# Interleaving the 128 rows of each streamed weight block's DRAM copy by sixteen

## The chip, the cores and the metric

The kernel runs on one core of one Trainium2 chip. The metric is device time in microseconds (us) of one execution. The kernel before was timed three times; the median is 1813.09 us.

## What is computed

Two blocks share the input `x` (2048 rows of 1024, bf16), after one layer norm, and their results are added to it:

```python
xn = _layernorm(x, axis=-1)
return x + _A_ref(xn, A_mem0, A_Wq, A_Wk, A_Wv, A_Wo, A_seg_len) + _B_ref(xn, ...)
```

Block A cuts the 2048 rows into 64 segments of 32. In front of each segment stand 8 rows of memory. The 40 rows go through attention with 32 heads of 128 (projections `Wq`, `Wk`, `Wv` of 1024 x 4096 each, then `Wo` of 4096 x 1024). The first 8 rows of the result are the memory of the next segment, so the 64 segments are a chain. Block B picks the two rows of `xn` with the largest product with `w_r`, runs them through a gated feed-forward layer (1024 to 3584 and back), and adds the result to these two rows.

## The kernel before

**The weights as granules.** The four matrices of block A are cut into 64 granules of 128 partitions x 2048 bf16 values (512 KB). Granules 0 to 47 hold 128 rows of half of `Wq`, `Wk` or `Wv`; granules 48 to 63 hold two heads of `Wo`. Every segment needs all 64 in a fixed order. 44 of them stay in SBUF (`resident`), three more are kept in PSUM and other corners (`KEPT_HERE`), and 17 are fetched again in each segment: the list `streamed` on line 80. One of these, granule 58 (`PART`), has 320 of its columns at home, so 432 KB of it travel.

**The copies.** In the original matrices a row of a granule is a piece of a longer row, or two pieces. So during segment 0 the program copies each streamed granule once, DRAM to DRAM, to a tile of its own, `wsc[g]` (line 123), whose 128 rows of 4,096 bytes lie one behind the other. `copy_block` (lines 442 to 444) issues these copies from GpSimd (POOL): six granules inside phase 1 of segment 0 (line 840), six after phase 1 and the last five after phase 2 (line 616).

**The stream.** `fetch` (lines 399 to 413) takes the next granule off the list `flow`, takes one of five slots (`wstream`, `N_SLOT = 5`) and issues one DMA from SyncE (SP) into it: in segment 0 from the original matrix, afterwards from `wsc[g]` (lines 407 and 412). `after` (line 622) calls `fetch` when TensorE (PE) has been given the last matmul that reads a streamed granule. The DMA waits until that granule's slot has been read, and for an earlier DMA of the same semaphore.

**One segment.** Lines 814 to 831 project the 32 rows that depend on the chain: six phases of eight granules, four matmuls of 128 x 512 each (line 821). Transposes, scores, softmax and attention are hooked in between. Lines 882 to 903 multiply with `Wo` (line 876). Besides the stream, GpSimd issues a few small transfers in each segment: the segment's rows of `x` (`XN`, line 354), queries, keys and values of the memory rows that were worked out ahead (`QKL`, line 637; `VL`, line 642), partial results (`ol_d`, line 664) and the output (line 909).

**Transfers of the form that the change brings in.** Three loads already read DRAM with 16 as the outer count and 8 rows inside, into 128 partitions: `left_rows` (line 223, tile `XLR`, at the start) and `load_left_x` (line 652, tile `XLS`, in the last segment), both 16 x 8 rows of 2,048 bytes of `x`, and `load_vl` (line 642, with two more from SP on line 588), 16 x 8 pieces of `vl_d`. In all three the sixteen groups stand 64 KB apart in DRAM, and the eight rows of a group follow each other.

Of the kernel before, what the change touches and what calls it, by code (L numbers as in the profile page):

```python
# [8 lines left out]
BF16 = mybir.dt.bfloat16  # L9
# [13 lines left out]
PART, AT_HOME = 58, 320  # L23
# [8 lines left out]
def kernel(  # L32
# [16 lines left out]
    nc = tc.nc  # L49
    P = 128  # L50
    Bsz, S, D = A_x.shape
# [28 lines left out]
    streamed = [1, 4, 11, 15, 21, 23, 29, 34, 37, 41, 45, 47, 50, 54, 56, 58, 63]  # L80
# [4 lines left out]
    def granule_dram(g):  # L85
        if g < 48:
            p, kc = divmod(g, KC)
            mat, half = PHASES[p]
            return Wqkv[mat][kc * P:(kc + 1) * P, 2048 * half:2048 * (half + 1)]
        w = g - 48  # L90
        return Wo2[2 * w * P:(2 * w + 2) * P, :].rearrange("(hh e) d -> e hh d", hh=2)
# [11 lines left out]
    def granule_out(t, g):  # L103
        return t[:, :] if g < 48 else t.rearrange("p (hh d) -> p hh d", hh=2)
# [3 lines left out]
    dram = ctx.enter_context(tc.tile_pool(name="dram", bufs=1, space=DRAM))  # L108
# [11 lines left out]
    vl_d = [dram.tile([16, 16, XL, 2, P], BF16, name=f"vl_d{t}") for t in range(4)]  # L120
    ol_d = [dram.tile([P, 16, XL * H], BF16, name=f"ol_d{t}") for t in range(4)]

    wsc = {g: dram.tile([P, 2048 - AT_HOME if g == PART else 2048], BF16, name=f"wsc{g}") for g in streamed}
    r_d = dram.tile([1, S], BF16, name="r_d")

    res_tiles = {}
# [4 lines left out]
    def room(g, name):  # L131
        if g not in place:
            return home(g, [P, 2048], BF16, name)[:, :]
        tag, i = place[g]
        return areas[tag][:, i, :]
# [14 lines left out]
    def travelling(g):  # L150
        if g != PART:
            return [(slice(0, 2048), granule_dram(g))]
        w = granule_dram(g)
        return [(slice(0, D - AT_HOME), w[:, 0, AT_HOME:D]), (slice(D - AT_HOME, 2048 - AT_HOME), w[:, 1, :])]
# [44 lines left out]
    for s in range(4):  # L199
        nc.vector.tensor_copy(out=SELM[:, s, 0:XM, :],  # L200
                              in_=IDENT[:, 32 * s:32 * s + XM].unsqueeze(2).to_broadcast([P, XM, 4]))
# [197 lines left out]
    def fetch():  # L399
        if not flow:  # L400
            return
        s, g = flow.pop(0)
        t = wstream.tile([P, 2048], BF16, tag="g", name="g")
        if g == PART and s < NSEG - 1:
            n = 2048 - AT_HOME
            for c, w in travelling(g) if s == 0 else [(slice(0, n), wsc[g][:, :])]:
                nc.sync.dma_start(out=t[:, c], in_=w)
            t = (OP, t)
        elif s == 0 or g == PART:
            nc.sync.dma_start(out=granule_out(t, g), in_=granule_dram(g))  # L410
        else:
            nc.sync.dma_start(out=t[:, :], in_=wsc[g][:, :])
        queued.append((g, t))

    def part(t, jq):
# [25 lines left out]

    def copy_block(g):
        for c, w in travelling(g):
            nc.gpsimd.dma_start(out=wsc[g][:, c] if g == PART else granule_out(wsc[g], g), in_=w)

    to_copy = list(streamed)
    flow += [(s, g) for s in range(NSEG) for g in (streamed if s else first_streamed) if s or g != GUEST]
# [44 lines left out]
    for g in range(KC):  # L492
        if g in first_streamed:
            assert flow.pop(0) == (0, g)
            t = wstream.tile([P, 2048], BF16, tag="g", name="g")
            queued.append((g, t))
        else:
            t = res_tiles[g] = room(g, f"wres{g}")
# [10 lines left out]
    for g in range(KC, 32):  # L509
        if g == GUEST:  # L510
            t = res_tiles[g] = room(v_homes[8], "guest")
            nc.sync.dma_start(out=t, in_=granule_dram(g))
        elif g in first_streamed:
            if len(queued) < N_SLOT:
                fetch()
        else:
            load_resident(g)
        if g >= 8 and g < 15:
            load_x(g - 7)
# [70 lines left out]
    def left_done(p):  # L590
        for g in range(8 * p, 8 * (p + 1)):
            if g in first_streamed and g != GUEST:
                fetch()
        if p == 0:
            sd_rows(MV[:, 1:NT, :], VE[:, 1:NT])
            spread(1, NT)
            router_tiles()
        elif p == 1:
            res_tiles.pop(GUEST)
            load_resident(v_homes[8])  # L600
            area("big0", [P, 8, 2048], "W8A")
            for g in AREAS["big0"]:
                load_resident(g)
        elif p == 2:
            router_top()
            route_rows()
        elif p == 3:
            route_turns(*routed[0])
            load_resident(hx)
            home_first()  # L610
        elif p == 4:
            area("big1", [P, 8, 2048], "W8B")
        elif p == 5:
            load_resident(hm)
        if p in (1, 2):
            copy_blocks(6)

    def copy_blocks(n):
        for _ in range(min(n, len(to_copy))):
            copy_block(to_copy.pop(0))  # L620

    def after(s, g):

        if g in streamed:
            fetch()
        if s == NSEG - 1:
            if g in resident and g < 48 and g not in place and g not in resident[:3]:
                free_homes.append(g)
            if g in (54, 55):
                for t in (2 * g - 108, 2 * g - 107):  # L630
                    load_left_x(t)
            if g >= 57:
                fetch_moe(1)
# [61 lines left out]
    for s in range(NSEG):  # L695
# [118 lines left out]
        for p, (mat, half) in enumerate(PHASES):  # L814
            PSm = psA.tile([P, 512], F32, tag="acc", name="PSm")
            behind = []
            for kc in range(KC):
                g = 8 * p + kc
# [249 lines left out]
```

## Time and profile before

| What | Value |
|---|---|
| three runs, median (lowest, highest) | 1813.09 us (1803.46, 1813.56) |
| the profiled execution, its own time | 1819.23 us |
| span of its instructions | 1817.6 us |
| granted TensorE clock, mean | 0.985 |
| bytes moved by DMA, mean rate | 673.33 MB, 370 GB/s |
| segments 1 to 63 in the trace | about 219 us to 1728 us |

The page's time strip divides the span into 40 equal slices: the first five are the loads and segment 0, the last two the work behind the last segment (block B's matrices and the rows computed ahead), and all between is the chain of segments. "DMA share" in a table of windows is the mean busy share of the core's 16 DMA engines. [...] "To landing" is the time from the issue of a DMA to its completion.

### The profile page before, as it was taken

The page shows a single profiled execution, that of the slowest core. Times are in us where ns is not written, and L with a number is a line of the kernel's source. Part 1 is how long each engine was busy: PE and PEld are TensorE (multiplying, and loading weights), DVE is VectorE, ACT ScalarE, POOL GpSimd, SP SyncE. Part 2 cuts the span into 40 slices and gives each one's busy share as a digit, 9 for nine tenths or more (in the row PEclk, how much of TensorE's full clock was granted, in tenths as well). Part 3 has the DMA queues.
Part 4 walks back from the last instruction along what each step waited for, and adds up shares of the span by engine and source line. Part 5 has one row for each costly group of instructions (what it writes and reads, how often), then busy time and mean ns, then how long its engine had stood idle before and what let it go on. Part 6 is the DMA issues. An engine that isn't in the chain of part 4 may idle for free. (4 is left out here: it accounts for less than half of the span.)

```text
span 1817.6 us, 70275 instructions
## 1 busy us (share of the span) xinstructions
PE 1564.2 (86%) x30261; PEld 840.5 (46%) x30273; DVE 887.0 (49%) x2843; ACT 779.6 (43%) x2027; POOL 330.6 (18%) x610
## 2 busy tenths in 40 slices
PE   8999888888888888888888888888888888888887
PEld 5444344444444444444444444444444444444454
DVE  6822255444555554545555554455555555555531
ACT  3343144444444444444444444444444444444410
POOL 1121311111111111111111111111111111111220
PEclk9999899999999999999999999999999999999999
DMA  9785999999999999999999999999999999999998
GB/s 357 281 291 174 304 366 381 357 384 378 382 387 389 390 397 368 389 388 389 396 387 383 393 381 366 382 396 393 395 394 395 372 388 393 396 394 393 397 379 294
DMA packets 215961, 673.33 MB, mean 370 GB/s; under 512 B 42801, under 2 KB 46433, under 8 KB 215649
## 3 DMA queue, kind: packets, MB, share of 16 engines
q1 hardware_dynamic: 189232, 616.61, 88.9%
q0 software_dynamic: 25392, 50.39, 8.2%
q8 instruction: 236, 3.87, 0.9%
q10 hardware_dynamic: 1024, 1.84, 0.3%
q14 instruction: 77, 0.62, 0.1%
HBM read 647.74 MB, written 29.81 MB: 373 GB/s over the span
## 5 line engine op out<-in xcount | busy, mean ns | idle before, releaser
L821 PE MATMUL PSm<-wres,ST 128*32 128x512 bf16 x6400 | 501.6, 383 | 0.0
L821 PEld LDWEIGHTS <-ST 128*32 128x32 bf16 x12288 | 314.9, 96 | 345.0 <-issue 105.1
L821 PE MATMUL PSm<-g,ST 128*32 128x512 bf16 x3080 | 306.9, 385 | 40.8 <-DMA g<-wsc 36.6
L435 ACT COPY BK<-KEPT 128x512 bf16<-128x512 bf16 x315 | 189.3, 601 | 179.7 <-PE WO L876 68.0
L876 PEld LDWEIGHTS <-OT 128*32 128x32 bf16 x8255 | 218.1, 98 | 85.3 <-issue 67.7
L830 ACT CAST XB<-PSm 128x512 bf16<-128x512 f32 x256 | 150.3, 587 | 116.0 <-PE PSm L821 114.1
L716 DVE COPY KT<-BT 128x512 bf16<-128x512 bf16 x126 | 51.0, 405 | 283.9 <-PE BT L706 283.8
L876 PE MATMUL WO<-W8B,OT 128*32 128x256 bf16 x4096 | 188.2, 279 | 0.0
L821 PE MATMUL PSm<-W8A,ST 128*32 128x512 bf16 x2048 | 182.3, 381 | 0.0
L637 POOL DMA_DIRECT2D QKL<-ql_d x63 | 46.8, 743 | 740.4 <-ACT OTL L789 724.4
L876 PE MATMUL WO<-g,OT 128*32 128x256 bf16 (+1 forms) x2497 | 130.8, 278 | 52.6 <-DMA g<-wsc 44.6
L909 POOL DMA_DIRECT2D out_dram<-XN x256 | 130.4, 517 | 181.2 <-DVE XN L905 168.4
L849 ACT CAST VM<-PSm 128x512 bf16<-128x512 f32 x128 | 79.6, 622 | 99.5 <-PE PSm L821 99.4
L435 DVE COPY BK<-KEPT 128x512 bf16<-128x512 bf16 x189 | 80.2, 424 | 72.6 <-ACT BK L435 36.8
L706 PEld LDWEIGHTS <-XB 128*128 128x128 bf16 x1024 | 57.8, 97 | 105.8 <-ACT XB L830 99.3
L706 PE MATMUL BT<-IDENT,XB 128*128 128x128 bf16 x1024 | 101.6, 222 | 2.5
L733 DVE TENSOR_TENSOR BS<-BS,CT 128x96 f32<-128x96 f32 (+1 forms) x256 | 59.6, 233 | 84.5 <-PE BS L726 80.0
L711 ACT COPY QT<-BT 128x512 bf16<-128x512 bf16 x128 | 75.0, 586 | 58.0 <-PE BT L706 55.6
L821 PE MATMUL PSm<-BK,ST 128*32 128x512 bf16 x567 | 77.0, 391 | 22.1 <-DVE ST L393 22.1
L534 PE MATMUL PSG<-XLT,wres 128*128 128x512 bf16 x336 | 93.1, 379 | 0.8 <-ACT GA L536 0.7
L751 DVE TENSOR_REDUCE DN<-BS 128x8 f32<-128x320 f32 x128 | 62.8, 491 | 60.0 <-ACT BS L743 60.0
L905 DVE CAST XN<-WO 128x256 bf16<-128x256 f32 x64 | 27.2, 424 | 132.8 <-PE WO L876 132.8
(195 smaller groups left out, 2339.1 us busy)
## 6 DMA issues: line engine op xcount, KB each, us to landing
g<-wsc SPq DMA_DIRECT2D x1008, 512.0 KB, 6.3
g<-wsc SPq DMA_DIRECT2D x62, 432.0 KB, 5.7
ql_d<-GA POOLq DMA_DIRECT2D x16, 512.0 KB, 6.7
QKL<-ql_d POOLq DMA_DIRECT2D x63, 128.0 KB, 6.3
MW<-in_B_w_gate_dram SPq DMA_DIRECT2D x16, 448.0 KB, 13.8
wres<-in_A_Wk_dram SPq DMA_DIRECT2D x12, 512.0 KB, 10.2
MW<-in_B_w_down_dram SPq DMA_DIRECT2D x12, 512.0 KB, 9.1
MW<-in_B_w_up_dram SPq DMA_DIRECT2D x12, 448.0 KB, 9.0
```

The lines of the kernel that those rows point to most:

```text
L435: copy(out=back[g][c], in_=KEPT_COLS[g][c])
L534: nc.tensor.matmul(PSG[:, :], lhsT=part(Gs[kc], h // 4)[:, P * (h % 4):P * (h % 4 + 1)], rhs=XLT[:, :, kc, :], start=(kc == 0), stop=(kc = ...
L706: nc.tensor.transpose(out=PTq[:, il, :, :].rearrange("p j r -> p (j r)"), in_=XB[:, il * P:(il + 1) * P], identity=IDENT[:, :])
L711: nc.scalar.copy(out=QT[half][:, :, :], in_=pv)
L716: (nc.vector.tensor_copy if s else nc.scalar.copy)(out=KT[half][:, :, 0:32], in_=pv)
L733: nc.vector.tensor_tensor(out=S4, in0=S4, in1=m, op=ALU.add)
L751: nc.vector.tensor_reduce(out=DN[:, :], in_=S8, axis=AX.X, op=ALU.add)
L821: nc.tensor.matmul(PSm[32 * jq:32 * jq + 32, :], lhsT=ST[:, kc, :], rhs=part(Gv, jq), start=(kc == 0), stop=(kc == KC - 1), tile_position= ...
L830: nc.scalar.copy(out=XB[:, :], in_=PSm[:, :])
L849: nc.scalar.copy(out=VM[half][:, :], in_=PSm[:, :])
L876: nc.tensor.matmul(PS[32 * g:32 * g + 32, c0:c1], lhsT=lhs(h), rhs=rhs, start=False, stop=(last and hs == 1), tile_position=(0, 32 * g), s ...
L909: nc.gpsimd.dma_start(out=out2[s * SEG:s * SEG + XM, 256 * g:256 * (g + 1)], in_=OB[32 * g:32 * g + XM, :])
```

## The change

Row numbers inside each copy change. The tile of a copy has now the shape 8 x 16 x columns, and all its users see it through a view with 16 in front: partition 8e + i of the granule (e from 0 to 15, i from 0 to 7) is row 16i + e of the copy. Before, partition p was row p. So what stood in eight rows that follow each other stands in eight rows that are 16 rows (64 KB) apart, and the sixteen rows 16i to 16i + 15 belong to sixteen blocks of eight partitions.

```diff
-    wsc = {g: dram.tile([P, 2048 - AT_HOME if g == PART else 2048], BF16, name=f"wsc{g}") for g in streamed}
+    wsc = {g: dram.tile([P // 16, 16, 2048 - AT_HOME if g == PART else 2048], BF16,
+                        name=f"wsc{g}").rearrange("i e c -> e i c") for g in streamed}
...
-            for c, w in travelling(g) if s == 0 else [(slice(0, n), wsc[g][:, :])]:
+            for c, w in travelling(g) if s == 0 else [(slice(0, n), wsc[g])]:
...
-            nc.sync.dma_start(out=t[:, :], in_=wsc[g][:, :])
+            nc.sync.dma_start(out=t[:, :], in_=wsc[g])
...
     def copy_block(g):
         for c, w in travelling(g):
-            nc.gpsimd.dma_start(out=wsc[g][:, c] if g == PART else granule_out(wsc[g], g), in_=w)
+            if g < 48 or g == PART:
+                nc.gpsimd.dma_start(out=wsc[g][:, :, c], in_=w)
+            else:
+                for hh in range(2):
+                    nc.gpsimd.dma_start(out=wsc[g][:, :, D * hh:D * (hh + 1)], in_=w[:, hh, :])
```

No engine's order changes, and all of SP's DMAs stand where they stood. The copies of granules 50, 54, 56 and 63 are two DMAs each where they were one. On GpSimd, in segment 0 behind phase 2, the rows before are these (the last number is the shape of what is written; `wsc_117` to `wsc_121` are the copies of granules 50, 54, 56, 58 and 63):

```order
L316 DMA RT_1345<-in_A_x_dram 1x16x64
L444 DMA wsc_117<-in_A_Wo_dram 256x1x1024
L444 DMA wsc_118<-in_A_Wo_dram 256x1x1024
L444 DMA wsc_119<-in_A_Wo_dram 256x1x1024
L444 DMA wsc_120<-in_A_Wo_dram 128x704
L444 DMA wsc_120<-in_A_Wo_dram 128x1024
L444 DMA wsc_121<-in_A_Wo_dram 256x1x1024
L567 COPY CT<-VG 128x4
```

In the changed program the same place reads:

```order
L317 DMA RT_1345<-in_A_x_dram 1x16x64
L449 DMA wsc_117<-in_A_Wo_dram 16x8x1024 x2
L449 DMA wsc_118<-in_A_Wo_dram 16x8x1024 x2
L449 DMA wsc_119<-in_A_Wo_dram 16x8x1024 x2
L446 DMA wsc_120<-in_A_Wo_dram 16x8x704
L446 DMA wsc_120<-in_A_Wo_dram 16x8x1024
L449 DMA wsc_121<-in_A_Wo_dram 16x8x1024 x2
L572 COPY CT<-VG 128x4
```

Nothing moved past anything else; four DMAs are added in front of the copy to `CT`.

## The prediction

> **What bounds the kernel now.** I read the page first: busy times, the strip by slices and the DMA queues.
>
> ```profile
> PE 1564.2 (86%) x30261; PEld 840.5 (46%) x30273; DVE 887.0 (49%) x2843; ACT 779.6 (43%) x2027; POOL 330.6 (18%) x610
> DMA  9785999999999999999999999999999999999998
> q1 hardware_dynamic: 189232, 616.61, 88.9%
> g<-wsc SPq DMA_DIRECT2D x1008, 512.0 KB, 6.3
> g<-wsc SPq DMA_DIRECT2D x62, 432.0 KB, 5.7
> ```
>
> Two rows run close to full. PE is busy for 86% of the span. The DMA strip shows 9 in every slice of the chain of segments, and SP's queue alone (q1) fills 88.9% of the sixteen engines' time. Of its 616.61 MB, 1008 x 0.524 + 62 x 0.442 = 556 MB are the reads that the change rearranges. To see which of the two ends the segments, I took the table of windows for the whole stretch of reads from the copies, and the waits inside it.
>
> ```profile
> 219.00:1728.00 1509.00, 1285.72 (x28178) 690.34 (x28175) 772.27 (x2569) 702.72 (x1881) 280.01 (x507) 0.99 1.01 386
> PE WO L876 <- DMA g<-wsc: 44.1, 111, 1.6
> PE PSm L821 <- DMA g<-wsc: 36.6, 91, 1.5
> L642 POOL DMA_DIRECT2D VL<-vl_d x63: 532/554/566, 232.4 to 1713.9; - x63
> ```
>
> The last three numbers of the window row are the clock, the DMA share and GB/s: a share of 1.01, so the engines are never out of work for long, at 386 GB/s. PE waits for granules 202 times, 80.7 us in total. The load of VL comes once a segment, so a segment takes (1713.9 - 232.4) / 62 = 23.90 us. It moves 16 x 512 + 432 KB of stream and 128 + 64 + 48 + 64 + 4 x 12 KB of other things, 9.19 MB; at 386 GB/s that is 23.8 us. So bytes over rate gives the segment: **the DMA engines set the pace**, and what the change is worth is what it does to the 386 GB/s. One per cent of the rate is 15 us.
>
> **How much rate there is to win.** I compared stretches of the same trace.
>
> ```profile
> 114.00:120.00 6.00, 5.87 (x53) 2.28 (x52) 0.00 (x0) 3.92 (x6) 0.50 (x1) 1.00 1.03 415
> 1000.00:1006.00 6.00, 5.30 (x112) 2.49 (x108) 1.75 (x6) 2.97 (x6) 1.65 (x3) 1.00 1.03 410
> 1007.00:1011.00 4.00, 3.44 (x88) 1.43 (x80) 3.10 (x11) 1.61 (x4) 0.00 (x0) 1.00 1.02 375
> 1760.00:1783.00 23.00, 22.84 (x154) 14.62 (x156) 1.28 (x2) 1.10 (x4) 0.56 (x1) 1.00 1.03 407
> ```
>
> The first row loads `Wv` from rows 8 KB apart, the fourth block B's matrices from rows 7 KB apart. Neither lies as the copies do, and they run at 415 and 407 GB/s. The second row is the stream from the copies with little beside it: 410 GB/s. The third, in the same segment, is the stream while GpSimd's loads of XN and VL land: 375. So the old layout already reads as fast as any other wherever it is undisturbed. Against the best stretch it lacks 5 of 415, 1.2%, which is 18 us over 1509 us; that is the most that a smoother order could take from quiet stretches. The rest of the way from 386 to 410 is lost beside other transfers, whose layout stays.
>
> **The change part by part.**
>
> *The reads, 1070 of them.* Same bytes, same rows of 4,096 (3,456) bytes, same slots, same waits. What changes is which rows are near each other in time. "The engines read rows that lie together" needs engines that stand at the same row at the same moment. A read lands 6.3 us after its issue, and one is issued every 23.90 / 17 = 1.41 us, so 4.5 are under way at once, and nothing in the program holds the sixteen engines together within them. An engine that is a few rows ahead reads another 64 KB, or another granule. No view shows engine positions, so this is an argument, not a reading. Price, bounded from both sides: -18 us (all of the quiet stretches' lack) to +0 from locality alone. I take 0, since the three layouts above differ by no more than their neighbours do.
>
> [...]
>
> *The issue on SP.* A read whose DRAM side is 16 x 8 needs longer on SP. The trace has the form on lines 588, 223 and 652:
>
> ```profile
> L412 SPq DMA_DIRECT2D g<-wsc x1008: 319/320/1404, 218.9 to 1728.3; - x168
> L588 SPq DMA_DIRECT2D VL<-vl_d x2: 533/538/542, 165.4 to 196.4; - x2
> L223 SPq DMA_DIRECT2D XLR<-in_A_x_dram x2: 573/637/701, 0.9 to 1.7; - x2
> L652 SPq DMA_DIRECT2D XLS<-in_A_x_dram x4: 599/662/870, 1728.7 to 1731.0; - x4
> ```
>
> I take the quiet 538 ns: 0.218 us more for each, 17 x 0.218 = 3.7 us of SP's time in a segment. SP then issues for 17 x 0.538 = 9.1 of 23.9 us, so it does not become a bound. Behind a late read stand only later reads of the stream, and for them waits PE. The cover is the queue: 4.5 reads under way are 6.3 us of work, and a read that enters 0.2 us later finds the engines busy (share 1.01). Cost 0. Without the cover, a slot's cycle of 5 x 1.41 = 7.05 us would grow by 0.218, 3.1%, or 47 us: the upper bound.
>
> *The copies on POOL.* Four DMAs more.
>
> ```profile
> L444 POOL DMA_DIRECT2D wsc<-in_A_Wo_dram x6: 692/940/1147, 129.2 to 131.9; - x6
> L444 POOL DMA_DIRECT2D wsc<-in_A_Wv_dram x5: 517/518/527, 92.5 to 97.7; - x5
> 129.23 3.85 POOL L444 DMA_DIRECT2D wsc<-in_A_Wo_dram  x6
> 158.02 0.19 POOL L567 COPY CT<-VG 128x4 bf16<-128x4 bf16 x1 [24.94 <-DVE PT L749]
> ```
>
> Six issues take 3.85 us; ten of half the pieces take between 10 x 0.518 = 5.2 us and 3.85 + 4 x 1.147 = 8.4 us. POOL's next work stood still for 24.94 us until 158, so 1.4 to 4.6 us disappear there. Cost 0; if the cover were gone, 4.6 us. The copies write the same bytes, and their first reader starts at 219 us, more than 80 us later.
>
> *The work behind the last segment* (40 us) is untouched.
>
> **The sum.** The profiled execution took 1819.23 us, 1.6 us of it outside its span of 1817.6, and stands 0.3% above the median of 1813.09. Terms: reads 0 (-18 to 0), issue 0 (0 to +47), copies 0 (0 to +4.6). So 1819 against its own time, and **1813 us** against the median.
>
> **Rivals.**
>
> *A: the form itself is slow (much slower).* The three transfers of the form 16 x 8 into 128 partitions are also the slow places of the trace:
>
> ```profile
> 4.00:7.00 3.00, 3.00 (x53) 3.00 (x51) 2.32 (x6) 0.00 (x0) 2.04 (x4) 1.00 1.05 253
> 12.00:15.00 3.00, 2.09 (x10) 1.01 (x9) 2.62 (x9) 0.21 (x1) 0.00 (x0) 0.50 1.07 391
> 1737.00:1743.00 6.00, 5.27 (x38) 3.34 (x30) 3.00 (x8) 0.00 (x0) 3.68 (x8) 0.88 1.05 282
> ```
>
> While XLR lands, full engines move 253 GB/s, and right afterwards 391; while XLS lands, 282. If the form does that, for instance because engine e then writes eight partitions in a row and two engines press on the same part of SBUF, every segment pays: 9.19 MB at 282 GB/s are 32.6 us, 8.7 us more, x 63 = +548 us, 2361 us. It decides as soon as the stream falls below PE's own 1285.72 / 63 = 20.4 us a segment, that is 450 GB/s, so at once. Against it: in these transfers the sixteen groups stand 64 KB apart, and after the change neighbouring groups stand 4 KB apart, so distance explains the slow places as well as form; and the slowdown reaches transfers of other forms that run beside them. I keep it at 0.10.
>
> [...]
>
> *B: faster.* The sixteen blocks of a granule now differ in their place inside 64 KB, whatever the engines' positions, the opposite of XLS. If crowding of engines on equal places is part of what slows the disturbed stretches, these get shorter. A third of the way from 386 to 410 GB/s gives 1509 x (1 - 386/394) = 31 us, 1782 us. PE's 80.7 us of waits for granules leave room for that. Against it: the disturbers keep their layout. 0.17.
>
> *C: slower by a little.* The issue time is not covered in the stretches where the queue runs low, or an engine pays for rows 64 KB apart: the 47 us above, 1860 us, as the far end, half of it, 1837 us, as the likely one. Against it: the share of 1.01. 0.10.
>
> *D: the change does nothing of what it says*, since the engines are not in step. That is the forecast itself, 0.63.
>
> **How the numbers follow.** Forecast 1813 us, with a range of its own of 1796 to 1829. A measurement of this kernel can tell about 1% from no change. Faster by over 1%: B, 0.17. Within 1%: 0.63. Slower: A and C, 0.20. For 8 in 10 I take in B down to 1782 and C up to 1845, and leave out A and the outer end of C.
>
> **What would show it.** Right: the window over the chain of segments again reads 386 within 4 GB/s, a segment takes 23.9 within 0.2 us, the issue on SP reads near 0.54 us, and PE's waits for granules stay near 80 us. Wrong by A: the window falls to 250 to 300 GB/s at a share above 1, PE's waits grow to several hundred us. Wrong by B: 390 or more, with PE's waits down to about 50 us. Wrong by C: a DMA share below 1 and reads that land less than 6 us after their issue.

## The result and the profile after

The change makes the kernel much slower. Seven executions of it, timed in turns with the kernel before on one chip, have a median of 2546.68 us (2508.34 to 2578.71), against 1816.99 us (1803.46 to 1821.41) for the kernel before. Their ratio is 1.3875, with a 95% interval of 1.3812 to 1.3938. It is worked out from the executions within 1.5% of the fastest, three of the seven here, so it lies a little below the ratio of the medians. The profiled execution, 2578.71 us with a span of 2577.0 us, is the longest of the seven. The forecast was 1813 us in a range of 1782 to 1845.

The page of the changed kernel, the rows that answer to those shown of before:

```profile
PE 1876.0 (73%) x30261; PEld 931.1 (36%) x30273; DVE 893.1 (35%) x2843; ACT 795.4 (31%) x2027; POOL 331.4 (13%) x614
PEclk9998788889888797788888788777878887888789
DMA  9769999999999999999999999999999999999998
q1 hardware_dynamic: 189232, 616.61, 92.8%
g<-wsc SPq DMA_DIRECT2D x1008, 512.0 KB, 9.9
g<-wsc SPq DMA_DIRECT2D x62, 432.0 KB, 9.6
```

SP's queue moved exactly as many packets and bytes as before (189232 and 616.61 MB), and the DMA strip is as full. But a read lands 9.9 us after its issue where it took 6.3, and PE's share fell from 86% to 73%. The window over the chain of segments (the last three columns are the clock, the DMA share and GB/s), the issue of the reads on SP, the load of `VL` that comes once a segment, and PE's waits for granules:

```profile
219.00:2480.00 2261.00, 1593.16 (x28135) 779.27 (x28130) 775.38 (x2560) 716.71 (x1874) 277.15 (x502) 0.82 1.03 257
```

```profile
L413 SPq DMA_DIRECT2D g<-wsc x1008: 514/514/935, 219.6 to 2484.4; - x168
L647 POOL DMA_DIRECT2D VL<-vl_d x63: 532/552/563, 235.7 to 2464.8; - x63
```

```profile
PE PSm L826 <- DMA g<-wsc: 422.6, 477, 3.1
PE WO L881 <- DMA g<-wsc: 187.7, 221, 2.7
```

The sixteen engines read as full as before (share 1.03, before 1.01), yet they move 257 GB/s where they moved 386. A segment takes (2464.8 - 235.7) / 62 = 35.95 us, where it took 23.90; 9.19 MB at 257 GB/s are 35.8 us. Over 63 segments the difference is 12.05 x 63 = 759 us, and the two profiled executions lie 2578.71 - 1819.23 = 759.5 us apart. So in this pair all of the loss stands in the stream. (By the ratio the loss is smaller, 0.3875 x 1816.99 = 704 us, since the profiled execution is the longest one.) PE's waits for granules grew from 80.7 to 610.3 us. PE itself was slower too: it was busy for 1593 us in the window where it was busy for 1286, at a granted clock of 0.82 where it was 0.99. That is not what sets the pace, since 1593 / 63 = 25.3 us stays far below 35.95.

The text on record names three things that would show rival A: a window of 250 to 300 GB/s, a share above 1, and waits of several hundred us. All three are there. What remained open is which property of the new reads is to blame: the form (16 groups of 8 rows), the 64 KB between the rows of a group, or the interleaved order.

### The profile page after: what moved, and what is told of

It is laid out like the page before. It is cut to its first block, busy times and chain, and to the rows that moved or that the text cites. A ratio compares the mean times of both kernels' runs of the same rounds, so it can differ in the third digit from the quotient of the medians.

```text
span 2577.0 us, 70280 instructions
## 1 busy us (share of the span) xinstructions
PE 1876.0 (73%) x30261; PEld 931.1 (36%) x30273; DVE 893.1 (35%) x2843; ACT 795.4 (31%) x2027; POOL 331.4 (13%) x614
## 3 DMA queue, kind: packets, MB, share of 16 engines
q1 hardware_dynamic: 189232, 616.61, 92.8%
## 4 chain that ended last, share of the span: by engine, by line
DMA 75%; PE 23%; issue 1%; DVE 1%; ACT 0%; POOL 0%; ACTq 0%; DVEq 0%; SPq 0%
DMA g<-wsc 74%; PE PSm L826 9%; PE PSG L539 4%; PE WO L881 4%; PE WD L955 2%; PE PSV L566 2%; PE BT L711 1%; DMA vl_d<-VG 1%; PE FIRST L252 0%; DMA XLR<-in_A_x_dram 0%; PE BT L370 0%; DMA out_dram<-XLS 0%; PE BS L783 0%; DMA wres<-in_A_Wq_dram 0%; DMA wres<-in_A_Wo_dram 0%
## 5 line engine op out<-in xcount | busy, mean ns | idle before, releaser
L826 PE MATMUL PSm<-g,ST 128*32 128x512 bf16 x3080 | 350.2, 441 | 425.6 <-DMA g<-wsc 422.6
L826 PEld LDWEIGHTS <-ST 128*32 128x32 bf16 x12288 | 338.9, 104 | 871.7 <-issue 699.0
L826 PE MATMUL PSm<-wres,ST 128*32 128x512 bf16 x6400 | 585.9, 441 | 0.0
L881 PEld LDWEIGHTS <-OT 128*32 128x32 bf16 x8255 | 267.4, 117 | 292.2 <-issue 243.5
L881 PE MATMUL WO<-g,OT 128*32 128x256 bf16 (+1 forms) x2497 | 166.6, 346 | 196.2 <-DMA g<-wsc 187.7
L881 PE MATMUL WO<-W8B,OT 128*32 128x256 bf16 x4096 | 237.9, 339 | 0.0
L826 PE MATMUL PSm<-W8A,ST 128*32 128x512 bf16 x2048 | 200.1, 415 | 0.0
L792 DVE CAST OT<-BT 128x128 bf16<-128x128 f32 x128 | 37.3, 291 | 219.7 <-PE BT L786 215.7
L826 PE MATMUL PSm<-BK,ST 128*32 128x512 bf16 x567 | 94.0, 505 | 22.2 <-DVE ST L394 22.2
L792 ACT CAST OT<-BS 128x128 bf16<-128x128 f32 x130 | 34.6, 266 | 240.4 <-PE BT L786 236.2
```

What stands on the lines that cost most here:

```text
L792: copy(out=OT[half][:, 2 * ph + jl, :, :], in_=ov[:, :, 0:SEG])
L826: nc.tensor.matmul(PSm[32 * jq:32 * jq + 32, :], lhsT=ST[:, kc, :], rhs=part(Gv, jq), start=(kc == 0), stop=(kc == KC - 1), tile_position= ...
L881: nc.tensor.matmul(PS[32 * g:32 * g + 32, c0:c1], lhsT=lhs(h), rhs=rhs, start=False, stop=(last and hs == 1), tile_position=(0, 32 * g), s ...
```

## The experiments

**forms: the disputed form by itself.** This kernel only issues transfers of 128 rows of 4,096 bytes from a weight matrix into eight tiles, one stretch for each form. `groups(n, m, pitch, k)` takes n groups of m rows, `pitch` rows apart. M is 24, N is 8 and P is 128, here and in the next two kernels of this kind:

```python
for k in range(M):
    nc.sync.dma_start(out=T[k % N][:, :], in_=R[P * (k % 16):P * (k % 16) + P, :])
...
    nc.sync.dma_start(out=T[k % N][:, :], in_=groups(16, 8, 9, k))
...
    nc.sync.dma_start(out=T[k % N][:, :], in_=R[P * (k % 16):P * (k % 16) + P, :].rearrange("(i e) c -> e i c", e=16))
...
    nc.sync.dma_start(out=T[k % N][32:96, :], in_=groups(8, 8, 9, k))
```

> This kernel leaves out the whole computation: it only loads rows of 4,096 bytes of Wq into SBUF, 24 transfers per stretch, one stretch after the other, and writes whatever lies in SBUF to the output. Stretches on SP: (1) 128 rows in order, a plain transfer; (2) the form 16 x 8 with rows in order, except that each group of 8 starts 9 rows behind the last; (3) 16 x 8 in the order of the change; (4) a plain transfer of 128 rows that are 64 KB apart; (5) 16 x 8 with the groups 64 KB apart, as XLR and XLS have it; (6) 32 x 4 and (7) 64 x 2, rows nearly in order; (8) 4 x 8 into partitions 0 to 31; (9) 8 x 8 into partitions 0 to 63; (10) 8 x 8 into partitions 32 to 95, from the same addresses; then from GpSimd (11) plain and (12) 16 x 8; last (13) plain from SP again. Theory 'form': with 16 in front of the DRAM side an engine is given eight partitions in a row, and the engines of partitions 0 to 31 and 32 to 63 press on the same part of SBUF. Then (2), (3), (5), (6), (7) run at 250 to 290 GB/s, (1) and (4) at about 400; (9) is slowed too but (10), which has no such pair, runs at twice (8). Theory 'order': the addresses do it, an engine's next row being 64 KB on. Then (2), (6), (7) run at about 400, (3), (4) and perhaps (5) at 250 to 290, and (9) and (10) are equal.

The windows over the stretches, in this order: 128 plain rows; 16 groups of 8 with rows in order; 16 groups of 8 in the order of the change; plain rows 64 KB apart; 16 groups of 8 with groups 64 KB apart; 32 groups of 4; 64 groups of 2; 4 groups of 8 into partitions 0 to 31; 8 groups of 8 into 0 to 63; the same into 32 to 95. Columns: length, busy DVE and POOL, clock, DMA share, GB/s.

```profile
8.00:30.00 22.00, 1.33 (x2) 0.00 (x0) 1.00 1.02 401
45.00:85.00 40.00, 0.00 (x0) 0.00 (x0) 1.00 1.03 240
100.00:140.00 40.00, 0.00 (x0) 0.00 (x0) 1.00 1.03 237
155.00:175.00 20.00, 0.00 (x0) 0.00 (x0) 1.00 1.02 403
192.00:232.00 40.00, 0.00 (x0) 0.00 (x0) 1.00 1.03 240
248.00:268.00 20.00, 0.00 (x0) 0.00 (x0) 1.00 1.03 412
283.00:303.00 20.00, 0.00 (x0) 0.00 (x0) 1.00 1.03 412
316.00:334.00 18.00, 0.00 (x0) 0.00 (x0) 1.00 0.26 105
350.00:372.00 22.00, 0.00 (x0) 0.00 (x0) 1.00 0.51 172
388.00:408.00 20.00, 0.00 (x0) 0.00 (x0) 1.00 0.51 210
```

Sixteen groups of eight run at 237 to 240 GB/s whatever the distance and order of their rows, and plain rows at 401 to 403, 64 KB apart too. (Issued from GpSimd, the two forms ran alike, at 237 and 409. The share passes 1.00 here with a single queue at work (1.03 on SP's alone), so the recorded times of one queue's own packets overlap.) So it is the form, and not the distance. It is not any form other than the plain one, though: 32 groups of 4 and 64 groups of 2 run at 412. There the expectation was wrong. Two readings lead further. Four groups keep a quarter of the engines busy (0.26), eight groups half of them (0.51), sixteen all. That fits one engine to each outer group, which then writes eight partitions in a row; no view names the engine of a packet. And the same eight groups run at 172 GB/s into partitions 0 to 63 and at 210 into 32 to 95, which is twice the 105 of four groups. The source is the same; **where the rows are written decides**.

The expectations of forms2 and forms3 make a theory of this, theory port. What it takes for granted of the engines and of their ways into SBUF, no view shows; what the two runs can show is the rate, and the time of a packet, at each place.

**form_only and order_only: the two halves of the change, each alone.** The first keeps the form of 16 groups of 8, with the rows in their old order (a gap of one row keeps the groups apart). The second keeps the plain form and puts the rows 64 KB apart. form_only is edited from the changed kernel and keeps its other edits, order_only from the kernel before.

```diff
+    wsc = {g: dram.tile([16, P // 16 + 1, 2048 - AT_HOME if g == PART else 2048], BF16,
+                        name=f"wsc{g}")[:, 0:P // 16, :] for g in streamed}
```

> The changed kernel with the copies' rows back in order (partition p follows partition p - 1), but each group of eight starting nine rows behind the last, so that the reads keep the form 16 x 8. Theory 'form': as slow as the change, 2450 to 2600 us, the chain of segments at 250 to 265 GB/s. Theory 'order': as before, 1800 to 1830 us at 386 GB/s.

```diff
-    wsc = {g: dram.tile([P, 2048 - AT_HOME if g == PART else 2048], BF16, name=f"wsc{g}") for g in streamed}
+    wsc = {g: dram.tile([P, 32768], BF16, name=f"wsc{g}")[:, 0:2048 - AT_HOME if g == PART else 2048] for g in streamed}
```

> The kernel before, with each row of a copy 64 KB behind the last one, so that the reads keep the plain form of 128 rows while an engine's next row is as far away as in the change. Theory 'form': as before, 1800 to 1830 us. Theory 'order', if an engine's own step of 64 KB is what costs: 2400 us or more.

form_only took 2432.17 us, a ratio of 1.3271 (1.3166 to 1.3376); order_only 1815.04 us, 1.0008 (0.9968 to 1.0049). The window over the reads of form_only, then that of order_only:

```profile
219.00:2350.00 2131.00, 1544.30 (x28193) 762.25 (x28193) 777.83 (x2572) 716.16 (x1885) 280.62 (x509) 0.85 1.03 273
```

```profile
219.00:1712.00 1493.00, 1282.63 (x28227) 686.87 (x28226) 773.23 (x2572) 703.13 (x1885) 281.40 (x510) 1.00 1.02 390
```

The form without the interleaving makes 0.327 of the loss of 0.388; rows 64 KB apart in the plain form cost nothing: 403 GB/s in forms, where rows in order gave 401, and the 1.0008 of order_only.

**form17: is it the 64 KB within the form?** The change and form_only differ by some 4%. In this kernel the rows of a group lie 68 KB apart in place of 64.

```diff
-    wsc = {g: dram.tile([P // 16, 16, 2048 - AT_HOME if g == PART else 2048], BF16,
-                        name=f"wsc{g}").rearrange("i e c -> e i c") for g in streamed}
+    wsc = {g: dram.tile([P // 16, 17, 2048 - AT_HOME if g == PART else 2048], BF16,
+                        name=f"wsc{g}")[:, 0:16, :].rearrange("i e c -> e i c") for g in streamed}
```

> The change with its groups of sixteen rows 17 rows apart in DRAM in place of 16, so that the eight rows of a group of the read lie 68 KB apart and not 64 KB. Theory pitch (the part of the loss that the form with rows in order does not show, ratio 1.3875 against 1.3271, comes from equal places 64 KB apart): 1.32 to 1.34 and 270 to 275 GB/s. Theory order (it comes from engines that read rows that lie together, whatever the distance): 1.37 to 1.40 and 255 to 260 GB/s.

It took 2515.78 us, 1.3827 (1.3731 to 1.3923), at 263 GB/s from 217 to 2430 us. Its interval overlaps that of the change (1.3812 to 1.3938) and not that of form_only (1.3166 to 1.3376). So the 4% do not come from the round distance; they come with the interleaved order, and only with the slow form, as the kernels with 32 and 64 below show.

**forms2 and forms3: which partitions collide.** Both again only move rows. The first places eight groups of 8 at four places, reads 32 x 4 and 64 x 2 interleaved, and writes SBUF to DRAM.

```python
for k in range(M):
    nc.sync.dma_start(out=T[k % N][0:64, :], in_=groups(8, 8, 9, k))
settle()
for k in range(M):
    nc.sync.dma_start(out=T[k % N][16:80, :], in_=groups(8, 8, 9, k))
...
```

> This kernel leaves out the whole computation: it only moves rows of 4,096 bytes, 24 transfers to a stretch, into eight tiles, and reads the rate of each stretch by itself. Theory port (an engine takes one outer group, that is eight partitions in a row, and two engines whose partitions lie 32 apart share a way into SBUF): of eight groups of eight, placed at partitions 0 to 63, four pairs collide, 172 GB/s as measured before; at 16 to 79 two pairs (the groups at 16 and 48, at 24 and 56 collide, and those at 32 and 64, 40 and 72 lie in another half), so between 180 and 200; at 32 to 95 none, 210; at 64 to 127 four pairs again, 172. A source of 32 groups of 4 or 64 groups of 2, here interleaved by 32 and by 64, runs as the plain one, 400 to 412. Theory descriptor (a source in 8 x 8 costs the engine more per row, whatever the destination): the four placements of 64 partitions within 5% of each other. Writing SBUF to DRAM: theory port has no measured row for it; if reading SBUF goes through the same way, the transfer into 16 groups of 8 rows runs near 240 and the plain one near 400; if only writing does, both run alike.

Eight groups at partitions 0, 16, 32 and 64, in this order:

```profile
42.00:72.00 30.00, 0.00 (x0) 0.00 (x0) 1.00 0.51 130
94.00:114.00 20.00, 0.00 (x0) 0.00 (x0) 1.00 0.51 208
128.00:148.00 20.00, 0.00 (x0) 0.00 (x0) 1.00 0.51 204
163.00:184.00 21.00, 0.00 (x0) 0.00 (x0) 1.00 0.51 193
```

The two places where the theory has no pair or few pairs are at full rate (204 at 32 to 95, 208 at 16 to 79), the other two below it, but not at the figures expected: 0 to 63 gave 130 where it had given 172, 64 to 127 gave 193, and 16 to 79 gave the full 208 where 180 to 200 was expected for its two pairs. The theory of the descriptors (no difference between places) falls; that of the ports needed a test without chance in it. A reading that would fit, and that no view shows: two groups that collide may fall out of step, and then neither waits. By the theory, sixteen groups of *four* rows leave no such escape: at partitions 0 and 64 all of them collide all the time, at 32 none do. (The other stretches: interleaved by 32 and 64, 398 and 408 GB/s; SBUF to DRAM, plain 420, in 16 groups of 8 rows 411, so reading SBUF in this form cost little here.)

```python
for p, n in ((0, 16), (32, 16), (64, 16), (0, 16), (32, 16), (64, 16), (32, 8), (0, 8), (64, 8), (16, 8), ...):
    for k in range(M):
        nc.sync.dma_start(out=T[k % N][p:p + 64, :], in_=groups(n, 64 // n, 64 // n + 1, k))
```

> This kernel leaves out the whole computation: it only moves rows of 4,096 bytes into tiles, 24 transfers to a stretch. Sixteen groups of 4 rows into 64 partitions, at 0, 32 and 64, each twice; eight groups of 8 rows at 32, 0, 64, 16, each twice; 64 plain rows at 0 and 32; then three times in turn 128 plain rows, 32 groups of 4 in order, and 32 groups of 4 interleaved by 32. Theory port (one engine to an outer group; partitions p and p + 32 of the same half share a way into SBUF): at 0 and at 64 the sixteen groups of 4 lie on eight ways and no luck of phase helps, so 200 to 215 GB/s at a share above 1 both times, and at 32 on sixteen ways, 390 GB/s or more (or what the issue of about 0.6 us for 262 KB lets through, with a share below 1). Eight groups of 8 at 32: 205 to 210 both times; at 0, 64 and 16 anything from 105 to 210, not twice the same, since two engines on one pair of ways may fall into step or out of it. Theory descriptor (the source's form alone costs): no difference between 0, 32 and 64. For the three forms into 128 partitions: if interleaving by 32 costs what the kernel with it lost (2%), it runs 5 to 10 GB/s below the 32 groups in order in all three rounds; if not, within 3 GB/s.

Sixteen groups of 4 at partitions 0, 32, 64 and 0, 32, 64 again; then eight groups of 8 at 0, at 64, at 0 and at 64; then 64 plain rows at 0 and at 32:

```profile
10.00:25.00 15.00, 0.00 (x0) 0.00 (x0) 1.00 1.04 208
41.00:51.00 10.00, 0.00 (x0) 0.00 (x0) 1.00 0.98 381
61.00:79.00 18.00, 0.00 (x0) 0.00 (x0) 1.00 1.04 209
95.00:113.00 18.00, 0.00 (x0) 0.00 (x0) 1.00 1.04 211
129.00:139.00 10.00, 0.00 (x0) 0.00 (x0) 1.00 0.98 375
150.00:167.00 17.00, 0.00 (x0) 0.00 (x0) 1.00 1.04 211
...
217.00:236.00 19.00, 0.00 (x0) 0.00 (x0) 1.00 0.51 204
252.00:278.00 26.00, 0.00 (x0) 0.00 (x0) 1.00 0.51 153
...
362.00:392.00 30.00, 0.00 (x0) 0.00 (x0) 1.00 0.51 132
413.00:444.00 31.00, 0.00 (x0) 0.00 (x0) 1.00 0.52 128
...
500.00:518.00 18.00, 0.00 (x0) 0.00 (x0) 1.00 1.03 208
534.00:544.00 10.00, 0.00 (x0) 0.00 (x0) 1.00 1.00 381
```

From the same source, sixteen groups of 4 move 208 to 211 GB/s into partitions 0 to 63 or 64 to 127 (share 1.04), and 375 to 381 into 32 to 95 (share 0.98); even 64 plain rows do so (208 and 381). Eight groups of 8 at 0, 64, 0 and 64 came out at 204, 153, 132 and 128; at 32 and 16 they gave 204 to 209 each time. The time that single packets of 4,096 bytes took in the trace says the same:

```
place, form                      packets   median ns
16 x 4 rows at partitions 0          762         322
16 x 4 rows at partitions 32         931         159
16 x 4 rows at partitions 64         917         320
8 x 8 rows at 32, first time         906         159
8 x 8 rows at 64, second time        970         276
the kernel before, 300 to 1500 us, mean          169
order_only, mean                                 169
form_only, mean                                  243
form17, mean                                     254
the change, mean                                 257
```

With sixteen groups of 4 a packet takes 159 ns at partitions 32, and twice as long at 0 and at 64, 322 and 320 ns. This is the collision as measured: the place alone makes it, and what lies behind it no view shows. The 16 x 8 form lies between, with 240 GB/s by itself, and with 257 to 273 GB/s and packets of 243 to 257 ns in the kernels. That this is a matter of step is the reading that fits the spread of 128 to 210 GB/s; no run sets the step by hand, so it is not shown.

The last nine stretches of forms3, three rounds of plain rows, 32 groups of 4 in order, and the same interleaved by 32, ran at 395, 404, 402; 405, 397, 402; 401, 405, 411 GB/s: interleaving by 32 costs nothing by itself.

**by32, order32, by64: the change's aim without the collision.** by32 and by64 interleave by 32 and 64 in place of 16; order32 has the 32 groups of 4 rows in the old order. All three keep the change's other edits.

```diff
+    wsc = {g: dram.tile([P // 32, 32, 2048 - AT_HOME if g == PART else 2048], BF16,
+                        name=f"wsc{g}").rearrange("i e c -> e i c") for g in streamed}
```

> The change with 32 in place of 16: the copies hold their rows interleaved by 32, and a read has 32 groups of 4 rows. Theory form (eight partitions in a row from one engine are what costs): 386 to 390 GB/s in the stretch of the reads and 1800 to 1825 us, a ratio of 0.99 to 1.01, since nothing else is left that costs, and nothing is won by rows that lie together. Theory interleaving (rows that lie together and are read by many engines at once cost by themselves, as the 4.5% between the change and the same form with rows in order may say): 3 to 5% slower, 1870 to 1910 us. Theory locality gains: 395 GB/s or more and 1780 us or less.

```diff
+    wsc = {g: dram.tile([32, P // 32 + 1, 2048 - AT_HOME if g == PART else 2048], BF16,
+                        name=f"wsc{g}")[:, 0:P // 32, :] for g in streamed}
```

> The kernel with the copies interleaved by 32, but with its 32 groups of 4 rows held in order, 5 rows apart. Theory interleaving (rows that lie together and are read by many engines at once cost 2%): this one runs as the kernel before, 0.995 to 1.005, 385 to 390 GB/s. Theory issue (513 ns for an issue on SP in place of 320 lets the queue run low: the share fell to 1.00): 1.015 to 1.03, 374 to 380 GB/s, as with interleaved rows.

```diff
+    wsc = {g: dram.tile([P // 64, 64, 2048 - AT_HOME if g == PART else 2048], BF16,
+                        name=f"wsc{g}").rearrange("i e c -> e i c") for g in streamed}
```

> The change with 64 in place of 16: interleaved by 64, 64 groups of 2 rows. Theory issue: as by 32, 1.015 to 1.03, since the issue is as long. Theory interleaving: with 64 the pairs of rows of a group lie 256 KB apart and neighbours still 4 KB; the same loss or a smaller one, 1.005 to 1.02. If neither costs, 0.995 to 1.005.

by32 took 1854.42 us, 1.0213 (1.0158 to 1.0269); order32 1862.21 us, 1.0272 (1.0226 to 1.0317); by64 1856.97 us, 1.0217 (1.0177 to 1.0256). So the big loss is gone with the groups of eight, and a loss of 39 to 49 us is left, where the theory of the form had none for by32. The window over the reads of by32, the issue on SP, then the window of order32:

```profile
215.00:1765.00 1550.00, 1297.09 (x28178) 690.45 (x28178) 772.24 (x2570) 704.03 (x1882) 280.49 (x507) 0.99 1.00 376
L413 SPq DMA_DIRECT2D g<-wsc x1008: 512/513/1364, 214.7 to 1765.2; - x168
```

```profile
215.00:1765.00 1550.00, 1295.68 (x28164) 685.30 (x28161) 771.74 (x2567) 704.78 (x1879) 279.59 (x505) 0.99 1.00 376
```

Rows in order lose as much as rows interleaved, so the theory of interleaving falls. Nor is the collision left: between 300 and 1500 us the mean packet takes 172 ns in all three, where it took 169 before, and half of them take 159 as before. What the three have in common is the read in groups, with an issue of 513 ns in place of 320, the term that the prediction had taken as covered, and 6.5 or 6.6 us from issue to landing in place of 6.3. Interleaving by itself wins nothing that these intervals can tell.

**forms4: is it the issue?** Forty transfers to a stretch go round n tiles, and a tile is free again when VectorE has read it.

```python
for n in (2, 3, 4, 5, 6, 8):
    for a in range(2):
        for form in (rows, lambda k: groups(32, 4, 5, k)):
            for k in range(40):
                nc.sync.dma_start(out=T[k % n][:, :], in_=form(k))
                if k >= n - 1:
                    for h in range(2):
                        nc.vector.tensor_copy(out=G[:, D * h:D * (h + 1)], in_=T[(k + 1) % n][:, D * h:D * (h + 1)])
            settle()
```

> This kernel leaves out the whole computation: 40 transfers to a stretch go round n tiles, and a tile is free again only when VectorE has read it (about 1.1 us for each, in the order of the transfers); n is 2, 3, 4, 5, 6, 8, and for each n the plain form and 32 groups of 4 rows take turns, twice. Theory issue (the 0.2 us more of the issue of a read with 32 groups counts only where the queue of the engines runs low, because a tile's next transfer starts that much later): with 2 and 3 tiles, where the round of a tile sets the rate, 32 groups are 3 to 6% below the plain form, about 0.2 of 4 to 5 us; with 6 and 8 tiles, where the engines are never out of work, within 1%; the crossing lies near 4 or 5. Theory form (32 groups of 4 cost the engines themselves 2%): the same 2% at every n, 8 too.

The windows come in pairs, plain and 32 groups; shown is the second pair of 2, 3, 4 and 5 tiles and the first of 6:

```profile
242.00:313.00 71.00, 21.40 (x56) 0.00 (x0) 1.00 0.63 207
345.00:424.00 79.00, 21.54 (x57) 0.00 (x0) 1.00 0.59 187
...
602.00:652.00 50.00, 21.39 (x56) 0.00 (x0) 1.00 0.86 293
677.00:731.00 54.00, 21.66 (x57) 0.00 (x0) 1.00 0.84 273
...
881.00:925.00 44.00, 21.62 (x57) 0.00 (x0) 1.00 0.95 345
948.00:992.00 44.00, 21.31 (x56) 0.00 (x0) 1.00 0.93 326
...
1123.00:1158.00 35.00, 21.14 (x56) 0.00 (x0) 1.00 1.02 408
1178.00:1214.00 36.00, 21.34 (x56) 0.00 (x0) 1.00 1.03 408
1231.00:1267.00 36.00, 21.33 (x56) 0.00 (x0) 1.00 1.03 411
1286.00:1323.00 37.00, 21.70 (x58) 0.00 (x0) 1.00 1.03 410
```

With 6 and 8 tiles the two forms run within 1 GB/s of each other, and with 5 nearly so (409 against 403 in the first pair); with 4, 3 and 2 tiles 32 groups are 5.5, 7 and 10% slower. So this form costs no rate while enough reads stand in line, and it costs as soon as the round of a tile sets the rate. The loss with few tiles is larger than the issue: with 3 tiles a round takes 3 x 0.524 MB / 293 GB/s = 5.37 us plain and 5.76 us with 32 groups, 0.39 us more, where the issue is 0.21 us longer. The instructions of this pair say where the rest is. From the start of an issue to VectorE's first read of the tile it is 4.58 us plain and 4.99 with 32 groups, and from the end of the issue still 4.25 and 4.45 (means over transfers 10 to 35). So half of the loss is the issue, and the other half a read that lands later once it is issued; why it does is open. VectorE holds the tile for 0.76 us in both (the expectation had 1.1). Here 5 tiles are enough; in the kernel other transfers share the engines (352 KB of a segment's 9.19 MB), PE holds a tile for longer (four matmuls of 385 ns on a projection granule, 1.54 us) and a read lands after 6.3 us, so that its five slots have less to spare. That the longer way from issue to landing is the whole of the 2 to 3% is an inference from the two, not a run.

**vl_any: another place of the slow form.** The load of `VL` is also cut in 16 pieces. This kernel reads the same 64 KB in one piece, which are not the segment's own, so the memory rows' part of the attention is computed from other data.

```diff
-        nc.gpsimd.dma_start(out=group["vl"][:, :, :], in_=vl_d[s // 16][:, s % 16, :, :, :])
+        nc.gpsimd.dma_start(out=group["vl"][:, :, :], in_=vl_d[s // 16][s % 16])
```

> The kernel before, its load of VL once a segment made one plain piece of 64 KB (same bytes, same tile): what it reads is not the segment's own, so the memory rows' part of the attention is computed from other data. Theory form (the load of VL in 16 groups of 8 rows is what slows the stream from 410 to 375 GB/s while it lands): that stretch goes up to 390 GB/s or more, and the kernel becomes 5 to 15 us faster, 0.99 to 0.997. Theory short packets (VL's 512-byte pieces and XN beside it slow the stream, whatever the form): no difference within 3 us, 0.998 to 1.002.

It took 1817.21 us, 1.0000 (0.9965 to 1.0036), and its window reads the 386 GB/s of before. Nothing is won. The load did become a plain one: the trace notes what each DMA writes as 128 x 1 pieces for the plain reads of the stream and as 1 x 128 for all reads in groups, and VL's went from the second to the first. In the 6 us behind its 63 issues the engines moved 381 GB/s on average where they moved 374, short of the 390 that the theory of the form asks for. The test is weak all the same: at 64 KB the load is an eighth of a read of the stream, and a gain of a few us lies within the interval.

No kernel here beats the one before: order_only stands level with it, and everything that gives the read a form of groups is slower.

## Why the prediction was wrong

- **The bound**: right. The DMA engines set the pace before and after, and bytes over rate gives the segment in both (23.8 for 23.90, 35.8 for 35.95 us).
- **The reads, taken as 0 "from locality alone": this is the step that failed.** As a price of locality it was right: order_only is at 1.0008, and order32 and by32, without and with interleaving, cannot be told apart. But the sum had one term for the reads, and the term held only the order of the rows. "Same bytes, same rows, same slots, same waits" left out what did change: the groups in which a read writes its partitions. In forms the outer count went with the busy share of the engines (0.26, 0.51 and 1.03 for 4, 8 and 16 groups), so the change did not only reorder rows. With 16 groups of 8 a packet takes 257 ns in place of 169; which engine then writes which partitions, no view names. So the term put at 0, with -18 to 0 as its bounds, was worth (35.95 - 23.90) x 63 = 759 us in the profiled pair. form_only, the form with the rows in order, makes 0.327 of the ratio's 0.388 by itself.
- **Rival A** named the form, and the signs that came, and got a chance of 0.10. The cause that it gives as an instance, two engines that press on the same part of SBUF, fits forms3 (208 GB/s into partitions 0 to 63, 381 into 32 to 95), but it was not shown, since no view names the engine of a packet. Two arguments had pulled it down. "Distance explains the slow places as well as form" falls with the 403 GB/s of plain rows 64 KB apart. "The slowdown reaches transfers of other forms that run beside them" never told the two apart: in the change, where the form is to blame, `QKL` keeps its own form and still lands after 8.0 us where it took 6.3. The two windows of this form in the trace of before, at 253 and 282 GB/s with full engines, were better evidence than the arguments against them.
- **A's size**: 2361 us, from the 282 GB/s of `XLS`. With the 253 GB/s of `XLR`, 9.19 MB take 36.3 us, 12.4 us more than before, and 1819 + 12.4 x 63 = 2600 us, close to the 2578.71 of the profiled execution. The window of `XLR` held little but this form (its four loads, issued from 0.9 to 1.7 us, landed 3.8 to 4.8 us later); in that of `XLS` loads of block B and of partial results ran beside it. That it comes so close is partly luck, since the rows of `XLR` are half as long.
- **The issue on SP, 0.538 us by the estimate**: measured 0.514. In the change bytes over rate gives the whole segment, so no cost of it shows there. The reason given was wrong all the same: "4.5 reads under way are 6.3 us of work" is no cover by itself. With the collision taken away, reads with the same issue cost 39 to 49 us, about the upper bound of 47 that the text had worked out and put aside; by forms4 the issue may be only half of that, and the later landing the rest. In forms4, 4 tiles read a share of 0.95 while the rate is 345 of 411 GB/s, so a share near 1 says less about the work in stock than I took from it.
- **The copies on POOL**: right. The ten issues of granules 50 to 63 took about 0.53 us each, and the first read was issued at 219.6 us, where it had been at 218.9.
- **B, the gain**: no run shows any. **C** has a far end of 47 us, near what by32 (39) and order32 (49) lose, but its signs are not there in them: by32 reads a share of 1.00, and its reads land after 6.5 us, not under 6.

## What to carry to other kernels

Look at the outermost count of the DRAM side of a transfer, and at the partitions on the other side, before anything else: in these runs the count went with the busy share of the engines (0.26, 0.51 and 1.03 for 4, 8 and 16 groups of 8), and the partitions with the rate (16 groups of 4 from the same source: 208 GB/s into 0 to 63, 381 into 32 to 95). If rows must be regrouped in DRAM, 32 x 4 and 64 x 2 kept 412 GB/s by themselves and cost 2 to 3% in this kernel; 16 x 8 fell to 237 to 240 and cost 33 to 39%. And when a trace already holds the form that a change brings in, price the change by those rows first, however short their windows are.

## What was not expected of the hardware

- Two forms that differ only in the outer count, 16 x 8 and 32 x 4, run at 240 and 412 GB/s into the same 128 partitions (forms); 64 plain rows run at 381 GB/s into partitions 32 to 95, into 0 to 63 at only 208 (forms3).
- The collision showed only where SBUF is written: into SBUF 16 groups of 8 rows ran at 240 GB/s, plain at 401 (forms); from SBUF to DRAM they ran at 411, plain at 420 (forms2).
- By itself the issue on SP is 0.33 us for a plain read, 0.54 us for one of 16, 32 or 64 groups and 0.60 to 0.68 us for one of 4 or 8 (forms). With 3 tiles in the round a read in 32 groups costs 0.39 us more, of which the issue is 0.21 (forms4).
- The engines' busy time for a byte was a tenth longer with fewer reads under way in forms4: with 4 tiles a share of 0.95 goes with 345 GB/s, with 8 tiles 1.03 with 411.
- The granted clock of TensorE fell with the slow stream: 0.82 in the window of the change and 0.85 in form_only, against 0.99 before and in by32, and 1.00 in order_only. The mean matmul on a streamed granule took 441 ns where it took 385. The matmuls were the same, with more idle time between them. Why the clock is lower is open, and it does not decide the time here.
- Still open: why interleaving costs some 4% more with 16 x 8 (1.3875 and 1.3827 against 1.3271) and nothing with 32 x 4.
